# Attention, two mixture-of-experts layers and a feed-forward layer on one core: how the values are loaded, where the row maximum is scaled, and which engine splits two weights

## The chip, the cores and the metric

The kernel runs on one core of a Trainium2 chip. The metric is the device time of one execution in microseconds (us); it includes everything from the first load to the last store.

## The reference

Three layers follow one another on 1536 tokens. First comes attention with 2 x 8 heads of 768 positions and 64 dimensions: each query sees the keys nearer than 16 positions and one summary for each block of 32 positions (the maximum of the keys, the mean of the values). Then every token goes to two of eight experts, and a dense layer with a squared ReLU ends it.

```python
k_sum = k.reshape(B, H, nb, block, D).max(axis=3)
v_sum = v.reshape(B, H, nb, block, D).mean(axis=3)
mask_l = np.abs(pos[:, None] - pos[None, :]) < window            # window 16, block 32
scores_s = scale * np.einsum('bhsd,bhnd->bhsn', q, k_sum) + np.log(block)
a = softmax(concat(where(mask_l, scale * q @ k.T, -1e9), scores_s))
x = a @ concat(v, v_sum)                                         # -> 1536 x 512
# experts: the two largest of 8 noisy logits per token
out[mask] += top2_w[mask, k, None] * (np.maximum(x[mask] @ w1[e], 0) @ w2[e])
# dense layer: s, b scalars
g = s * np.maximum(x @ w_in, 0)**2 + b;  y = g @ w_out
```

## The kernel before

**Attention** is tiled into 8 units, each one pair of heads, and each unit into two groups of 384 queries: 16 groups, n = 0 to 15, group n belonging to unit n // 2. For each unit SyncE's queue issues the loads of the transposed keys (`load_k`), queries (`load_q`) and values (`load_vT`), 128 rows of 768 float32 each, and of the values as the second product reads them (`load_vw`): a tile `VW` of 1560 columns (12 windows x 2 heads x 65, the 65th column holding ones). Of `VW` the rows 0 to 95 come by DMA, as two pieces of 768 columns a row and a third of 24 columns from an array of its own, `v_end`; rows 96 to 120 hold the sums of 24 blocks, which the kernel makes itself, and a row of 1e-9.

A group goes through these stages, each with its own function. `stage_s` (L732 and L735) multiplies queries with the 96 keys of a window and 24 block maxima, in PSUM. `stage_exp` takes the row maximum on VectorE (L742), scales it (L743), and ScalarE forms the exponentials in six instructions (L746). `stage_pt` transposes the result on TensorE (L756) and ScalarE brings it back (L760). `stage_pv` is the product with `VW` (L773), divided on VectorE (L776 and L778). The main loop runs these for groups n, n - 2 and n - 3 side by side. Beside them, for the next unit, `windows` (L709) copies the keys' windows on GpSimd, `block_max` (L713) takes the blocks' maxima on VectorE, and `place_ks` (L717) spreads them on GpSimd. `make_vsum` adds the values of a block: for units 0 to 3 one reduction on VectorE (L688), for units 4 to 7 five additions on GpSimd (L693). `place_vsum` brings the sums into `VW` (L698 on ScalarE, L699 on GpSimd).

Every engine and the SyncE queue run their instructions in the order of the program; that order is written out by hand. `extra(n)` stands at the end of group n: in the even groups it makes the windows of the next unit and issues the loads, `VW` of unit u + 1 first and then keys, queries and values of unit u + 2. A load of `VW` waits until the unit that used its buffer (there are three) is through `stage_pv`. SyncE issues a DMA only when the DMA eight before it has landed.

**The tables.** `CHUNK_AT` says in which groups the first three chunks of expert weights are loaded (`load_chunk`, two DMAs of 512 KB each). `SPLIT_AT` says in which groups `split_step` makes of a weight block a rounded part and a remainder, each for two 128 x 512 halves: ScalarE rounds (L490 and L491), GpSimd subtracts (L492 and L493). The splits 0 and 1 read chunk 0, the splits 2 and 3 chunk 1. `GATE_EV` says whether VectorE (1) or ScalarE (0) takes a transposed token block of the gate out of PSUM (`gate_t`). `ROUTE` spreads the routing of the first half of the tokens, VectorE work for the most part, over groups 12 to 15; it ends with nine comparisons `ohb` (L268). `TAIL` is the order of the work behind the last group, in which the rest of the attention, the routing of the second half (`t`, `u`, `r`, `o`, `i`) and the first expert's steps (`l1`, `l2`) are interleaved; `s.4` there is split 4, `x.1`, `g.5`, `m.1` and `z.1` are a transposition of gathered tokens and the gate. Behind `TAIL` run the experts and the dense layer, where TensorE has no gap.

Of the kernel before, what the change touches and what calls it, by code (L numbers as in the profile page):

```python
# [9 lines left out]
F32 = mybir.dt.float32  # L10
# [9 lines left out]
DRAM = bass.MemoryType.DRAM  # L20

EDGE_CAP = 256
GATE_EV = {(1, 1): 0, (1, 3): 1, (1, 5): 0, (0, 1): 0, (1, 0): 1, (0, 4): 0, (1, 4): 1}
CHUNK_AT = (7, 9, 12)
SPLIT_AT = (12, 13, 14, 15)
SPLIT_DVE = {8: 1, 9: 1, 4: 0}
ROUTE = {12: 2, 13: 3, 14: 7, 15: 6}
GATE = {(10, 0): 't0', (10, 1): 't1', (10, 2): 't2', (11, 0): 't3 m0', (11, 1): 't4', (11, 2): 't5 z0', (12, 0): 'm1', (12, 1): 'z1'}
XT_B = 4
TAIL = ("pt.1 pv.0 d.0 pt.2 pv.1 g.0 g.1 pv.2 g.2 g.3 m.0 x.0 g.4 z.0 x.1 g.5 m.1 l1.0 z.1 l1.1 t.0 s.4 l2.0 l1.2 u.0 c.3 l2.1 s.5 "  # L30
        "r.0 o.7 l2.2 o.2 s.6 l1.3 l1.4 l2.3 o.2 s.7 l1.5 l2.4 c.4 i.0 l1.6 s.8 l1.7 s.9 l2.6 l2.5 p.0 p.1 e.0 p.2 p.3 l2.7 l1.8")
MID_CAPS = (464, 440, 424, 416, 392, 368, 344)


@with_exitstack
def kernel(ctx: ExitStack, tc, q, k, v, v_end, vt_in, w_gate, w_noise, noise, w1, w2,
                      w_in, w_out, s_in, b_in, out):
    nc = tc.nc
    N, Dm = out.shape
    B, H, S, D = 2, 8, N // 2, 64  # L40
# [24 lines left out]
    cp = ctx.enter_context(tc.tile_pool(name="cp", bufs=1))  # L65
# [7 lines left out]
    bk23 = pp.tile([P, 2, 512], F32, name="bk23")  # L73
# [20 lines left out]
    for h in range(2):  # L94
        d = identb[64 * h:64 * h + 64]
# [8 lines left out]
        nc.vector.tensor_copy(masks[kind], masks[0])  # L104
        nc.vector.memset(masks[kind][:, lo:lo + 16], NEG)
    ident = cp.tile([P, P], F32, name="ident")
    zero6 = cp.tile([P, 2, 3], F32, name="zero6")
    wgn = cp.tile([P, DT, 32], F32, name="wgn")
    nz_in = cp.tile([P, B, NI, E], F32, name="nz_in")
    sb_in = cp.tile([P, 2], F32, name="sb_in")  # L110
# [300 lines left out]
    def split_step(n, eng=nc.vector):  # L411
# [11 lines left out]
        split(t, r1[:, :, j * P:(j + 1) * P], r2[:, j], eng)  # L423

# [59 lines left out]
        eng.tensor_tensor(out=v2[:, 1], in0=w, in1=v2[:, 0].bitcast(F32), op=OP.subtract)  # L484


    def split(t, a, bb, eng=nc.vector):

        v4 = t.rearrange("p a (t n) -> p a t n", n=P)
        nc.scalar.activation(v4[:, 0], a, AF.Copy)  # L490
        nc.scalar.activation(t[:, 1], bb, AF.Copy)  # L491
        eng.tensor_tensor(out=v4[:, 2], in0=a, in1=v4[:, 0].bitcast(F32), op=OP.subtract)  # L492
        eng.tensor_tensor(out=t[:, 3], in0=bb, in1=t[:, 1].bitcast(F32), op=OP.subtract)  # L493

# [169 lines left out]
    def win4(t):  # L664
        return t.rearrange("p (j h d) -> p j h d", h=2, d=D + 1)

    def load_k(u):
        kT[u] = kTb[u % 2]
        nc.sync.dma_start(kT[u][:, KPAD:KPAD + S], k[u])

    def load_q(u, eng=nc.sync):
        qT[u] = ap_.tile([P, S], F32, name="qT", bufs=3)
        eng.dma_start(qT[u], q[u])

    def load_vT(u):
# [164 lines left out]
    for t in VW:  # L840
        v4 = win4(t)
        nc.gpsimd.memset(v4[96:KW + 1, :, :, D:D + 1], 1e-9)
        nc.gpsimd.memset(v4[96:KW, :, :, D:D + 1], 32.0)
# [308 lines left out]
    with tc.If(n_over > 0):  # L1152
# [50 lines left out]
```

## Time and profile before

| | |
|---|---|
| three runs | 698.17, 699.72, 700.32 us; median 699.72 us |
| the profiled execution | 702.6 us, of which the span from the first to the last instruction is 700.8 us |
| TensorE, matmuls | 657.2 us busy, 94% of the span |
| VectorE, ScalarE, GpSimd | 441.1, 360.3 and 173.1 us busy |
| granted clock of TensorE | 0.977 of full speed on average |
| DMA | 96 MB in 59,817 packets, of which 7,592 under 512 bytes |

Times in the rows below are microseconds from the start of the span. PE is TensorE's matmuls, PEld its weight loads, DVE VectorE, ACT ScalarE, POOL GpSimd, SPq SyncE's queue. An average over the span says little here: the first 131 us are attention and routing, and the rest is experts and dense layer.

### The profile page before, as it was taken

What the parts mean: (1) busy time and instruction counts of PE and PEld (TensorE: products, weight loads), DVE (VectorE), ACT (ScalarE), POOL (GpSimd) and SP (SyncE); (2) the same over time, 40 slices, a digit from 0 to 9 for tenths busy, and PEclk for the clock granted to TensorE, in tenths of its full rate; (3) what the DMA queues carried; (4) which work ended last, traced back from release to release, by engine and by line L of the source; (5) the groups of instructions that cost most, each with busy time, mean ns of one, the idle gap of its engine ahead of it and who ended that gap; (6) DMA issues with size and microseconds to landing.
All of it is one profiled execution on the core that took longest, in us unless ns stands there. A gap on an engine that the chain in (4) does not pass through costs nothing.

```text
span 700.8 us, 11245 instructions
## 1 busy us (share of the span) xinstructions
PE 657.2 (94%) x4236; PEld 574.0 (82%) x4236; DVE 441.1 (63%) x765; ACT 360.3 (51%) x667; POOL 173.1 (25%) x204
## 2 busy tenths in 40 slices
PE   3796589899999999999999999999999999999995
PEld 3675468788999999999988897888888888888884
DVE  3754938566677677676777766788654565544542
ACT  3684624444545455455656566556454454444431
POOL 5364927403204131221313153610500000000000
PEclk9996789999999999999999999999999999999998
DMA  8898151775556566566667651510410000100001
GB/s 229 246 262 296 63 182 61 235 257 166 189 178 223 194 198 205 192 206 213 220 208 253 225 155 42 178 61 30 121 60 1 1 0 1 60 1 1 0 1 64
DMA packets 59817, 95.99 MB, mean 137 GB/s; under 512 B 7592, under 2 KB 34216, under 8 KB 59756
## 3 DMA queue, kind: packets, MB, share of 16 engines
q1 hardware_dynamic: 55611, 82.02, 36.0%
q0 software_dynamic: 4144, 13.18, 6.8%
q8 instruction: 35, 0.57, 0.3%
q14 instruction: 27, 0.21, 0.1%
HBM read 82.01 MB, written 13.17 MB: 136 GB/s over the span
## 4 chain that ended last, share of the span: by engine, by line
PE 84%; DMA 7%; DVE 5%; SPq 1%; ACT 1%; issue 1%; POOL 0%; DVEq 0%; ACTq 0%; POOLq 0%
PE sbk L499 38%; PE bk L520 24%; PE bk L934 13%; DMA VW<-in_v_dram 3%; PE mbk L526 3%; DMA qT<-in_q_dram 2%; PE mbk L520 1%; PE mbk L965 1%; DMA kT<-in_k_dram 1%; PE bk L773 1%; DVE ohb L268 1%; PE mbk L756 1%; PE mbk L804 1%; DMA xg<-x_d,ids_i 1%; DMA r<-in_moe_w_dram 0%
## 5 line engine op out<-in xcount | busy, mean ns | idle before, releaser
L499 PE MATMUL sbk<-xh,w 128*128 128x512 f32 (+8 forms) x960 | 278.9, 355 | 0.0
L499 PEld LDWEIGHTS sbk<-xh,w 128*128 128x128 f32 x960 | 175.4, 188 | 19.4 <-ACT xh L528 0.4
L499 PE MATMUL sbk<-xl,w 128*128 128x512 f32 (+8 forms) x480 | 170.4, 355 | 0.2 <-DVE xl L529 0.2
L520 PE MATMUL bk<-w,hh 128*128 128x512 f32 (+2 forms) x512 | 161.0, 396 | 0.0
L520 PEld LDWEIGHTS bk<-w,hh 128*128 128x128 f32 (+2 forms) x512 | 93.5, 188 | 17.8
L459 POOL TENSOR_TENSOR cl<-cl,cp 128x512 f32<-128x512 f32 x32 | 41.2, 1289 | 250.5 <-DVE cp L458 234.5
L520 PE MATMUL bk<-w,hl 128*128 128x512 f32 (+2 forms) x256 | 100.5, 392 | 0.0
L499 PEld LDWEIGHTS sbk<-xl,w 128*128 128x128 f32 x480 | 90.3, 188 | 10.3 <-DVE xl L529 0.5
L934 PE MATMUL bk<-hh,w 128*128 128x464 f32 (+4 forms) x320 | 96.3, 362 | 0.0
L490 ACT ACTIVATE w<-r 128x512 fp32r<-128x512 f32 x72 | 45.5, 633 | 85.1 <-PE bk L934 57.8
L492 DVE TENSOR_TENSOR w<-r,w 128x512 fp32r<-128x512 f32 x64 | 44.2, 691 | 37.3 <-ACT w L490 37.0
L510 ACT ACTIVATE yr<-sbk 128x512 f32<-128x512 f32 x48 | 28.7, 598 | 71.2 <-PE sbk L499 71.2
L515 DVE SCALAR_TENSOR_TENSOR hl<-yr,sb_in,hh 128x512 fp32r<-128x512 f32 x48 | 40.0, 833 | 36.0 <-ACT hh L512 36.0
L511 DVE SCALAR_TENSOR_TENSOR yr<-yr,sb_in 128x512 f32<-128x512 f32 x48 | 36.0, 750 | 41.9 <-ACT yr L510 41.9
L934 PEld LDWEIGHTS bk<-hh,w 128*128 128x128 f32 x320 | 59.8, 188 | 2.5
L512 ACT ACTIVATE hh<-yr,sb_in 128x512 fp32r<-128x512 f32 x48 | 34.8, 725 | 45.9 <-DVE yr L511 45.9
L484 DVE TENSOR_TENSOR w<-wres,w 128x1024 fp32r<-128x1024 f32 x36 | 44.1, 1224 | 22.1 <-ACT w L483 22.1
L520 PEld LDWEIGHTS bk<-w,hl 128*128 128x128 f32 (+2 forms) x256 | 47.8, 187 | 11.9 <-DVE hl L515 0.8
L934 PE MATMUL bk<-hl,w 128*128 128x464 f32 (+4 forms) x160 | 56.9, 356 | 0.0
L503 ACT ACTIVATE hh<-sbk 128x256 fp32r<-128x256 f32 (+7 forms) x72 | 34.5, 479 | 42.0 <-PE sbk L499 39.7
L483 ACT ACTIVATE w<-wres 128x1024 fp32r<-128x1024 f32 x39 | 41.3, 1059 | 14.4 <-PE bk L520 9.6
L504 DVE SCALAR_TENSOR_TENSOR hl<-sbk,hh 128x256 fp32r<-128x256 f32 (+7 forms) x72 | 38.9, 541 | 10.5 <-ACT hh L503 10.3
(190 smaller groups left out, 873.9 us busy)
## 6 DMA issues: line engine op xcount, KB each, us to landing
r<-in_moe_w_dram SPq DMA_DIRECT2D x72, 512.0 KB, 4.5
c<-in_moe_w_in_dram SPq DMA_DIRECT2D x16, 512.0 KB, 3.8
c<-in_moe_w_out_dram SPq DMA_DIRECT2D x16, 512.0 KB, 3.7
y_d<-yr SPq DMA_DIRECT2D x23, 256.0 KB, 2.2
VW<-in_v_dram SPq DMA_DIRECT2D x8, 576.0 KB, 11.1
kT<-in_k_dram SPq DMA_DIRECT2D x8, 384.0 KB, 8.3
qT<-in_q_dram SPq DMA_DIRECT2D x8, 384.0 KB, 10.2
xl<-in_vT_dram SPq DMA_DIRECT2D x8, 384.0 KB, 9.8
```

The lines of the kernel that those rows point to most:

```text
L459: nc.gpsimd.tensor_tensor(out=lf, in0=lf, in1=pw.bitcast(F32), op=OP.mult)
L483: nc.scalar.activation(v2[:, 0], w, AF.Copy)
L484: eng.tensor_tensor(out=v2[:, 1], in0=w, in1=v2[:, 0].bitcast(F32), op=OP.subtract)
L490: nc.scalar.activation(v4[:, 0], a, AF.Copy)
L492: eng.tensor_tensor(out=v4[:, 2], in0=a, in1=v4[:, 0].bitcast(F32), op=OP.subtract)
L499: nc.tensor.matmul(ps, wgt[:, t], x[:, t], start=i == 0, stop=i == 3 * DT - 1)
L504: nc.vector.scalar_tensor_tensor(out=hl, in0=ps, scalar=0.0, in1=hh.bitcast(F32), op0=OP.max, op1=OP.subtract)
L511: nc.vector.scalar_tensor_tensor(out=r2, in0=r, scalar=sb_in[:, 0:1], in1=r, op0=OP.mult, op1=OP.mult)
L512: nc.scalar.activation(hh, r2, AF.Identity, bias=sb_in[:, 1:2])
L515: nc.vector.scalar_tensor_tensor(out=hl, in0=r2, scalar=sb_in[:, 1:2], in1=hh.bitcast(F32), op0=OP.add, op1=OP.subtract)
L520: nc.tensor.matmul(a, g, wgt, start=first and j == 0, stop=last and j == 2)
L934: nc.tensor.matmul(a[:, 0:C], wgt[:, c], x[:, 0:C], start=f == 0 and j == 0, stop=last and j == 2)
```

## The change

The values are laid out on the host as 128 whole rows of 1560 columns, with the ones, the 32s and the 1e-9 of column 65 already in them, so that `load_vw` is one DMA of 128 x 1560 float32 instead of two of 96 rows, and the memory sets of these columns on GpSimd fall away. The loads of `VW` go behind the keys, queries and values of the unit after (at the start: behind the keys and queries of units 0 and 1). Rows 96 to 120 are now written by the DMA first and by `place_vsum` after it. The row maximum is written to a few columns of the group's own PSUM bank and scaled from there. All block sums are one reduction on VectorE. Splits 0 and 1 move from groups 12 and 13 to 6 and 8 and run on GpSimd alone; splits 2 and 3 move from groups 14 and 15 into `TAIL`. Chunks 0, 1, 2 are loaded in groups 3, 7, 12 instead of 7, 9, 12. Three of the six blocks of the first gate are taken out of PSUM by VectorE instead of ScalarE. The core of the diff:

```diff
-GATE_EV = {(1, 1): 0, (1, 3): 1, (1, 5): 0, (0, 1): 0, (1, 0): 1, (0, 4): 0, (1, 4): 1}
-CHUNK_AT = (7, 9, 12)
-SPLIT_AT = (12, 13, 14, 15)
+GATE_EV = {(0, 1): 1, (0, 3): 1, (0, 5): 1, (1, 0): 1, (1, 3): 1, (1, 4): 1}
+CHUNK_AT = (3, 7, 12)
+SPLIT_AT = (6, 8)
...
-TAIL = ("pt.1 ... g.4 z.0 x.1 g.5 m.1 l1.0 z.1 l1.1 t.0 s.4 ...
+TAIL = ("pt.1 ... g.4 z.0 x.1 s.2 g.5 m.1 l1.0 z.1 s.3 l1.1 t.0 s.4 ...
...
-    def split(t, a, bb, eng=nc.vector):
+    def split(t, a, bb, eng=nc.vector, hi=act_copy):
         v4 = t.rearrange("p a (t n) -> p a t n", n=P)
-        nc.scalar.activation(v4[:, 0], a, AF.Copy)
-        nc.scalar.activation(t[:, 1], bb, AF.Copy)
+        hi(v4[:, 0], a)
+        hi(t[:, 1], bb)
         eng.tensor_tensor(out=v4[:, 2], in0=a, in1=v4[:, 0].bitcast(F32), op=OP.subtract)
         eng.tensor_tensor(out=t[:, 3], in0=bb, in1=t[:, 1].bitcast(F32), op=OP.subtract)
...
     def load_vw(u):
-        nc.sync.dma_start(VW[u % 3][0:96, 0:2 * S].rearrange("p (t n) -> p t n", t=2), v[u].rearrange("t p n -> p t n"))
-        nc.sync.dma_start(VW[u % 3][0:96, 2 * S:], v_end[u])
+        nc.sync.dma_start(VW[u % 3], v[u])
     def make_vsum(u):
-        if u < HP:
-            nc.vector.tensor_reduce(z[:, 96:KW], t, AX.X, OP.add)
-            return
-        w = 16
-        while w:
-            dst = t[:, :, 0:w] if w > 1 else z[:, 96:KW, None]
-            nc.gpsimd.tensor_tensor(out=dst, in0=t[:, :, 0:w], in1=t[:, :, w:2 * w], op=OP.add)
-            w //= 2
+        nc.vector.tensor_reduce(z[:, 96:KW], t, AX.X, OP.add)
...
-        nc.vector.tensor_reduce(mx, ps, AX.X, OP.max, negate=True)
-        nc.vector.scalar_tensor_tensor(out=mx, in0=mx, scalar=SCALE, in1=zero6, op0=OP.mult, op1=OP.add)
+        m = (bk23, bk45)[n % 2][:, 0, 3 * KW:3 * KW + 6].rearrange("p (h i) -> p h i", h=2)
+        nc.vector.tensor_reduce(m, ps, AX.X, OP.max, negate=True)
+        nc.vector.tensor_single_scalar(mx, m, SCALE, op=OP.mult)
...
     load_q(0)
+    load_k(1)
+    load_q(1)
     load_vT(0)
-    load_k(1)
     load_vw(0)
-    load_q(1)
     load_vT(1)
...
-            if 1 <= u < NU - 1:
-                load_vw(u + 1)
             if u + 2 < NU:
                 load_k(u + 2)
                 load_q(u + 2)
                 load_vT(u + 2)
+            if 1 <= u < NU - 1:
+                load_vw(u + 1)
...
-        for c in range(4):
-            if SPLIT_AT[c] == n:
-                split_step(c, nc.gpsimd)
+        if n in SPLIT_AT:
+            split_step(SPLIT_AT.index(n), nc.gpsimd, nc.gpsimd.tensor_copy)
```

In the rows that follow, a number behind a name is a buffer's, and the brackets name what an instruction waits for: DMAHW a landing, PE, DVE, Activation, Pool the engine.

SyncE's queue, the loads of units 2 to 4, before (`r1`, `r2` would be a chunk's two halves; chunk 0 stands 14 rows further down):

```order
L680 DMA VW2_149<-in_v_dram 96x2x768 [waits DMAHW5_49]
L681 DMA VW2_149<-in_v_end_dram 96x24 [waits DMAHW6_49]
L669 DMA kT1_146<-in_k_dram 128x768 [waits DMAHW7_49,DVE_49,Pool_49]
L673 DMA qT_357<-in_q_dram 128x768 [waits DMAHW0_49,PE_49]
L677 DMA xl_152<-in_vT_dram 128x768 [waits DMAHW1_49,DVE_49]
L680 DMA VW0_147<-in_v_dram 96x2x768 [waits DMAHW2_49,PE_49]
L681 DMA VW0_147<-in_v_end_dram 96x24 [waits DMAHW3_49]
L669 DMA kT0_145<-in_k_dram 128x768 [waits DMAHW4_49,DVE_49,Pool_49]
L673 DMA qT_488<-in_q_dram 128x768 [waits DMAHW5_49]
L677 DMA xl_152<-in_vT_dram 128x768 [waits DMAHW6_49,DVE_49]
```

The same place after:

```order
L671 DMA kT1_145<-in_k_dram 128x768 [waits DMAHW3_49,DVE_49,Pool_49]
L675 DMA qT_345<-in_q_dram 128x768 [waits PE_49]
L679 DMA xl_151<-in_vT_dram 128x768 [waits DMAHW6_49,DMAHW5_49,DVE_49]
L682 DMA VW2_148<-in_v_dram 128x1560
L407 DMA r1_412<-in_moe_w1_dram 128x4x256 [waits DMAHW7_49]
L408 DMA r2_413<-in_moe_w2_dram 128x2x512 [waits DMAHW0_49]
L671 DMA kT0_144<-in_k_dram 128x768 [waits DMAHW1_49,DVE_49,Pool_49]
L675 DMA qT_479<-in_q_dram 128x768 [waits DMAHW2_49,PE_49]
L679 DMA xl_151<-in_vT_dram 128x768 [waits DMAHW3_49,DVE_49]
L682 DMA VW0_146<-in_v_dram 128x1560 [waits DMAHW4_49,PE_49]
```

Each `VW` moved behind the three loads of the unit after it, and chunk 0 came in ahead of unit 4's keys.

GpSimd, from the windows of unit 4 (group 6) to those of unit 5 (group 8), before; L699 is `place_vsum`, L693 the block sums:

```order
L709 COPY kw0_143<-kT0_145 128x12x96 [waits DMAHW4_49,PE_49,Pool_49]
L717 COPY kw0_143<-ks_612 128x12x24 [waits DVE_49]
L699 COPY VW0_147<-vs_652 25x24x64 [waits Activation_49,Pool_49]
L693 TENSOR_TENSOR xl_152<-xl_152 128x24x16 [waits DMAHW6_49,Pool_49]
L693 TENSOR_TENSOR xl_152<-xl_152 128x24x8 [waits Pool_49]
L693 TENSOR_TENSOR xl_152<-xl_152 128x24x4 [waits Pool_49]
L693 TENSOR_TENSOR xl_152<-xl_152 128x24x2 [waits Pool_49]
L693 TENSOR_TENSOR vz0_150<-xl_152 128x24 [waits PE_49,Pool_49]
L709 COPY kw1_144<-kT1_146 128x12x96 [waits DMAHW1_49,PE_49]
L717 COPY kw1_144<-ks_754 128x12x24 [waits DVE_49]
```

And after, where L703, L711 and L693 are the windows, the maxima and `place_vsum`:

```order
L703 COPY kw0_142<-kT0_144 128x12x96 [waits DMAHW1_49,PE_49,Pool_49]
L711 COPY kw0_142<-ks_604 128x12x24 [waits DVE_49]
L492 CAST w4_613<-r1_412 128x512 [waits DMAHW7_49]
L493 CAST w4_613<-r2_413 128x512 [waits DMAHW0_49]
L494 TENSOR_TENSOR w4_613<-r1_412,w4_613 128x512 [waits Pool_49]
L495 TENSOR_TENSOR w4_613<-r2_413,w4_613 128x512 [waits Pool_49]
L693 COPY VW0_146<-vs_648 25x24x64 [waits DMAHW4_49,Activation_49,Pool_49]
L703 COPY kw1_143<-kT1_145 128x12x96 [waits DMAHW5_49,PE_49,Pool_49]
L711 COPY kw1_143<-ks_746 128x12x24 [waits DVE_49]
```

Split 0 took the place of the block sums, and `place_vsum` now waits for the landing of its `VW` as well.

## Rows read from the trace of the kernel before

**Rows 1.** Stretches: borders, length, busy us of each engine, granted clock, DMA share, GB/s

```profile
31.65:39.87 8.22, 8.14 (x199) 7.05 (x199) 8.01 (x15) 6.97 (x25) 4.60 (x5) 1.00 0.74 221
55.23:68.70 13.47, 8.65 (x128) 6.77 (x128) 4.78 (x10) 6.73 (x21) 5.06 (x7) 0.59 0.86 273
68.70:82.40 13.70, 10.53 (x189) 9.14 (x191) 12.99 (x39) 9.71 (x30) 12.11 (x14) 0.87 0.35 113
82.40:92.70 10.30, 4.81 (x63) 4.08 (x59) 7.09 (x16) 3.03 (x8) 8.68 (x9) 0.54 0.07 17
131.00:700.00 569.00, 562.41 (x2825) 494.62 (x2823) 359.94 (x571) 293.25 (x480) 100.47 (x84) 0.99 0.39 125
```

**Rows 2.** Chain that ended last, in order of time: start, us, what

```profile
5.36 14.18 DMA VW<-in_v_dram
19.60 11.91 DMA qT<-in_q_dram
45.04 8.51 DMA kT<-in_k_dram
82.48 5.49 DVE ohb L268 x9
```

**Rows 3.** Timeline: start, us, what, idle before and its releaser

```profile
3.87 0.95 DVE L713 TENSOR_REDUCE ks<-kT 128x24 f32<-128x768 f32 x1
15.13 0.68 PE L732 MATMUL bk<-kw,qT 64*64 64x120 f32 x8 [5.21 <-DMA qT<-in_q_dram]
31.65 0.44 PE L732 MATMUL bk<-kw,qT 64*64 64x120 f32 x8 [2.73 <-DMA qT<-in_q_dram]
55.23 0.43 PE L732 MATMUL bk<-kw,qT 64*64 64x120 f32 x8 [0.23 <-POOL kw L717]
```

**Rows 4.** Stretches chosen by what the DMA queue carries, columns as in Rows 1

```profile
8.00:13.00 5.00, 1.07 (x13) 0.45 (x8) 3.87 (x6) 2.31 (x9) 2.06 (x3) 1.00 1.06 237
31.00:33.00 2.00, 1.35 (x39) 1.25 (x40) 1.93 (x4) 0.34 (x2) 1.49 (x2) 1.00 1.03 395
55.00:59.00 4.00, 1.05 (x39) 0.84 (x39) 3.37 (x6) 2.18 (x8) 3.62 (x6) 0.84 1.07 398
60.00:64.00 4.00, 2.94 (x23) 2.15 (x17) 0.00 (x0) 1.78 (x6) 0.00 (x0) 0.50 1.06 267
68.00:70.00 2.00, 2.00 (x26) 1.74 (x19) 1.93 (x10) 0.15 (x1) 1.27 (x2) 0.50 0.88 269
```

**Rows 5.** Scaling and division on VectorE, ns min/median/max; one scaling beside GpSimd

```profile
L743 DVE SCALAR_TENSOR_TENSOR mxs<-mxs,zero x16: 166/186/1307, 10.1 to 80.0; 128x6 f32<-128x6 f32 x16
L778 DVE TENSOR_TENSOR xs<-bk,rc x16: 557/557/558, 24.3 to 94.9; 128x384 f32<-128x384 f32 x16
...
31.08 1.47 POOL L699 COPY VW<-vs 25x1536 f32<-25x1536 f32 x1
31.25 1.31 DVE L743 SCALAR_TENSOR_TENSOR mxs<-mxs,zero 128x6 f32<-128x6 f32 x1
```

**Rows 6.** Groups by line from 31.65 to 39.87: busy us, mean ns, idle before

```profile
L746 ACT ACTIVATE sm<-bk,mxs 128x120 f32<-128x120 f32 x18 | 4.8, 372 | 3.3 <-DVE mxs L743 3.3
L760 ACT ACTIVATE PT<-mbk 121x384 f32<-121x384 f32 x6 | 2.8, 525 | 0.0
...
L688 DVE TENSOR_REDUCE vz<-xl 128x24 f32<-128x768 f32 x1 | 0.9, 944 | 0.0
```

**Rows 7.** VectorE: scalings by line from 66.9 to 88; second routing's comparisons

```profile
L743 DVE SCALAR_TENSOR_TENSOR mxs<-mxs,zero 128x6 f32<-128x6 f32 x3 | 2.3, 780 | 0.1
...
117.97 1.37 DVE L268 TENSOR_SCALAR ohb<-i,lo 128x128 f16<-128x128 f16 x7
```

**Rows 8.** GpSimd by line from 5 to 75, columns as in Rows 6

```profile
L709 POOL COPY kw<-kT 128x1152 f32<-128x1152 f32 x7 | 8.0, 1143 | 30.0 <-DMA kT<-in_k_dram 30.0
...
L492 POOL TENSOR_TENSOR w<-r,w 128x512 fp32r<-128x512 f32 x1 | 1.3, 1267 | 0.0
```

**Rows 9.** Timeline of the tail, ScalarE, between x.1 and m.1

```profile
100.33 0.60 ACT L794 ACTIVATE xt<-mbk 128x512 f32<-128x512 f32 x1
```

More of the change, by code (lines that the diff above doesn't have):

```diff
@@ L29 @@
 XT_B = 4
-TAIL = ("pt.1 pv.0 d.0 pt.2 pv.1 g.0 g.1 pv.2 g.2 g.3 m.0 x.0 g.4 z.0 x.1 g.5 m.1 l1.0 z.1 l1.1 t.0 s.4 l2.0 l1.2 u.0 c.3 l2.1 s.5 "
+TAIL = ("pt.1 pv.0 d.0 pt.2 pv.1 g.0 g.1 pv.2 g.2 g.3 m.0 x.0 g.4 z.0 x.1 s.2 g.5 m.1 l1.0 z.1 s.3 l1.1 t.0 s.4 l2.0 l1.2 u.0 c.3 l2.1 s.5 "
         "r.0 o.7 l2.2 o.2 s.6 l1.3 l1.4 l2.3 o.2 s.7 l1.5 l2.4 c.4 i.0 l1.6 s.8 l1.7 s.9 l2.6 l2.5 p.0 p.1 e.0 p.2 p.3 l2.7 l1.8")
@@ L35, with kernel @@
 @with_exitstack
-def kernel(ctx: ExitStack, tc, q, k, v, v_end, vt_in, w_gate, w_noise, noise, w1, w2,
+def kernel(ctx: ExitStack, tc, q, k, v, vt_in, w_gate, w_noise, noise, w1, w2,
                       w_in, w_out, s_in, b_in, out):
@@ L106 @@
     ident = cp.tile([P, P], F32, name="ident")
-    zero6 = cp.tile([P, 2, 3], F32, name="zero6")
     wgn = cp.tile([P, DT, 32], F32, name="wgn")
@@ L409, in load_chunk, with act_copy, split_step @@
         nc.sync.dma_start(r2, bb[:, f0:f0 + 2 * P, :].rearrange("o (t p) d -> p (o t) d", p=P))
-    def split_step(n, eng=nc.vector):
+    def act_copy(dst, src):
+        nc.scalar.activation(dst, src, AF.Copy)
+    def split_step(n, eng=nc.vector, hi=act_copy):
         if n >= len(steps):
@@ L422, in split_step @@
         j = n % 2
-        split(t, r1[:, :, j * P:(j + 1) * P], r2[:, j], eng)
+        split(t, r1[:, :, j * P:(j + 1) * P], r2[:, j], eng, hi)
     cv = {}
@@ L831 @@
         nc.vector.memset(t[:, :, :, KW:], 1.0)
-    nc.vector.memset(zero6, 0.0)
     windows(0, 0, 6, nc.scalar)
@@ L839 @@
     nc.gpsimd.memset(wgn, 0.0)
[L840 to L843, printed above, removed]
     st = {}
@@ L1157 @@
     main.close()
-_INS = ['q', 'k', 'v', 'v_end', 'vT', 'moe_w_gate', 'moe_w_noise', 'moe_noise', 'moe_w1', 'moe_w2',
+_INS = ['q', 'k', 'v', 'vT', 'moe_w_gate', 'moe_w_noise', 'moe_noise', 'moe_w1', 'moe_w2',
         'moe2_w_in', 'moe2_w_out', 'moe2_s', 'moe2_b']
@@ L1172, in layouts @@
     vp[:, :, 16:16 + S] = v.reshape(NU, 2, S, D)
-    vw = np.ones((NU, 96, NJ, 2, D + 1), v.dtype)
+    vw = np.zeros((NU, 128, NJ, 2, D + 1), v.dtype)
+    vw[:, :96, :, :, D] = 1.0
+    vw[:, 96:120, :, :, D] = 32.0
+    vw[:, 120, :, :, D] = 1e-9
     for j in range(NJ):
-        vw[:, :, j, :, :D] = vp[:, :, 64 * j:64 * j + 96].transpose(0, 2, 1, 3)
-    vw = vw.reshape(NU, 96, -1)
-    return qT, kT, vw[:, :, :2 * S].reshape(NU, 96, 2, S).transpose(0, 2, 1, 3), vw[:, :, 2 * S:], vT
+        vw[:, :96, j, :, :D] = vp[:, :, 64 * j:64 * j + 96].transpose(0, 2, 1, 3)
+    return qT, kT, vw.reshape(NU, 128, -1), vT
 def kernel(**inputs):
@@ L1187 @@
     inputs = dict(inputs)
-    inputs['q'], inputs['k'], inputs['v'], inputs['v_end'], inputs['vT'] = layouts(_np, *(inputs[n] for n in 'qkv'))
+    inputs['q'], inputs['k'], inputs['v'], inputs['vT'] = layouts(_np, *(inputs[n] for n in 'qkv'))
     for name in _INS:
```

## The prediction

> **What bounds the kernel now.** I read the stretches first. From 131 us to the end TensorE is busy 562.4 of 569 us [rows 1]; the change touches nothing there, so whatever it does must show earlier, and a microsecond won ahead of 131 us is won at the end. Next the chain in order of time: its long pieces up to 54 us are loads, 14.2 us behind a `VW`, 11.9 behind queries, 8.5 behind keys [rows 2]. The timeline says the same from TensorE's side: the scores of group 2 begin at 15.13 us after 5.21 us of waiting for queries, group 6 at 31.65 after 2.73 us [rows 3]; GpSimd waits 30 us in all for keys [rows 8]. So the first half is paced by one DMA queue. Only from group 6 to 9 are loads in time: 18 exponentials are three groups, 8.22 us, 2.74 a group, with VectorE busy 8.01 and ScalarE 6.97 of it [rows 1, 6]. [...]
>
> **Why the loads are slow.** The queue is full nearly always, but at two speeds. Where it carries transfers of 128 rows only (keys, queries, values, chunks, stores) it moves 395 to 398 GB/s; where `VW` is among them 237 to 267, and with a `VW` nearly alone 269, at the same busy share of about 1 [rows 4]. The trace does not say which part of `VW` costs that, the 96 rows or the 96-byte pieces of `v_end`; the change removes both. I take 395 for all loads after; the other end is 237, no cure at all, and in between `VW` at 269 with the rest at 395.
>
> [...]
>
> **Part 1, the loads.** A load of keys, queries or values is 128 x 768 x 4 = 0.393 MB, a `VW` 0.799 (0.599 before), a chunk 1.049, the first half's two stores 1.573. Unit 0's keys are in use at 3.87 [rows 3], which at 395 GB/s puts the stream's start at 2.85.
> - Group 2 needs the keys and queries of unit 1, now third and fourth, but VectorE first sums unit 0's values, fifth: 1.966 MB, 7.8 us. Then come three operations of 0.95 each (sum, maximum, block maximum [rows 3, 6]) and the scaling, 0.17 [rows 5]: 10.8, and with the placing on GpSimd 11.4 instead of 15.13.
> - The keys of unit 6 stand behind 13.65 MB in the new order (19 loads of 0.393, five `VW`, two chunks, small ones): 37.4 us. Before it was 12.2 MB, landed at 45.04 + 8.51 = 53.55 [rows 2], some 240 GB/s.
> - The values of unit 7 (they hold up VectorE now, since their sum runs there) stand behind 17.98 MB: 48.4 us.
>
> Single landings trail the stream by a microsecond or two, which I leave in the range.
>
> **Part 2, the pace.** If the loads are in time, a group costs 2.74 [rows 1]. The sum on VectorE for units 4 to 7 adds 0.94 per two groups [rows 6], and the scaling gives back: it takes 0.17 alone and up to 1.31 beside a GpSimd copy, whose end it shares (31.08 + 1.47 against 31.25 + 1.31), while the division, which reads one operand from PSUM, takes 0.557 always [rows 5]. From PSUM the scaling should therefore never wait; I price it at 0.17 to 0.2, and the maximum written into PSUM at its old 0.9. I take 2.85 a group. Groups 2 and 3 run at the lower clock as now (0.68 against 0.43 us for eight matmuls [rows 3]), 3.2 each. Group 10 then starts at 11.4 + 6.4 + 6 x 2.85 = 34.9; 10 and 11 with the gate take 4 each (two ScalarE copies of 0.6 more [rows 9]), so group 12 starts at 43 instead of 55.23. The keys (37.4 and 1.6 for windows and maxima) are earlier. **Gain 12.**
>
> **Part 3, from group 12 to the comparisons' end.** Before: 55.23 to 87.97, 32.7 us [rows 2, 3]. VectorE was busy 4.78 + 12.99 + 5.49 = 23.3 of it [rows 1, 2]. The splits leave GpSimd here, so the three slow scalings lose 1.8 (2.3 less 3 x 0.17), and the nine comparisons fall to what seven cost where GpSimd is quiet for most of them, 1.37: 1.8 instead of 5.5 [rows 7]. That is 17.8, and two sums of 0.94 make it 19.7. VectorE binds here, TensorE need not wait and keeps its clock. End at 43 + 19.7 = 62.7 instead of 87.97. The loads bound it lower: unit 7's values at 48.4 and the part of the VectorE work that stands behind them, some 11 of the 19.7 us by my estimate, give 60. **Gain 13 more, 25 in all.**
>
> **Part 4, the tail.** Split 2 now stands between `x.1` and `g.5`, where ScalarE is on the path: two copies of 128 x 512, 0.6 each by the nearest one [rows 9], 1.2 lost; split 3's copies fit beside `l1`. GpSimd's four subtractions of 1.27 [rows 8] move into the tail beside VectorE's second routing: 0 to 1.5 lost. Against it the stretch from 82.4 to 92.7 ran at a clock of 0.54 [rows 1] with TensorE half idle; without the wait a microsecond comes back. **Net loss 2** (0 to 3).
>
> **Part 5, costs at nothing, with their cover.** Splits 0 and 1 on GpSimd: two copies of 0.6 to 1.3 and two subtractions of 1.27 each [rows 8], about 4 us in groups 6 and 8. The cover is the 2.5 us of GpSimd sums that leave every unit from 4 on and the 30 us it now waits; without it the windows of the next unit are late by up to 4. Their chunk lands by 23.5 us (8.16 MB), ahead of group 6. ScalarE loses eight copies in groups 12 to 15, counted nowhere, since VectorE binds there.
>
> **Sum.** 25 - 2 = 23 us against the profiled 702.6: 679.6. The runs' median lies 2.9 below the profiled execution, so I expect **677**.
>
> **Rivals.**
> - *GpSimd's queue becomes the bound.* `place_vsum` now waits for its `VW`, which lands last of its unit, and the windows of the unit after stand behind it. For: unit 4's `VW` lands at 33.5 us (12.12 MB), split 1 holds GpSimd to about 36, then 1.47 and 1.14 and the maxima [rows 5, 8]: windows of unit 6 at 39.5, against 43 needed. Against: that margin of 3.5. If copies and landings are both slow it costs up to 6: 683.
> - *The loads stay the bound.* At 300 GB/s unit 7's values land at 62.8, and 11 us of VectorE behind them end at 74: a gain of 14 less 2, 688. With `VW` at 269 and the rest at 395, six `VW` (4.79 MB) take 17.8 us instead of 12.1 and unit 7's values land 5.7 later than 48.4: end at 65 instead of 62.7, 679.
> - *Slower.* 96 rows are not the cause, and the mixed rate stays. Then 1.5 MB more stand ahead of unit 6's keys, and unit 7's values land at 2.85 + 17.98 / 0.237 = 78.7, the comparisons end at 90, 2 later than now, and the tail adds 1 to 2: 703. It decides below some 250 GB/s. For: the slow seconds hold more than `VW`. Against: two fast stretches with 128 rows of other sizes [rows 4].
> - *It does nothing.* A gain of some 12 in the loads given back by GpSimd and by a lower clock: 700.
>
> [...]
>
> **How the numbers follow.** Forecast 0.62, GpSimd 0.15, loads 0.13, nothing 0.04, slower 0.06. The forecast's own range is 668 to 684: up to 9 us less if the end comes by the loads (60), the tail loses nothing and the slow routing operations beside GpSimd's splits, not counted above, shrink too; up to 7 more for late landings. With the first two rivals the range is 667 to 690. A difference of 0.3%, 2.1 us, can be told from none: faster 0.91, the same 0.04, slower 0.05.
>
> **What would show it.** Right: the DMA rate in the first 45 us near 390 with no slow stretch; group 2 at 11 to 12, group 12 at 42 to 45, comparisons done at 60 to 66; no scaling above 0.25 us; the clock at 1.0 from 20 us on. Wrong: GpSimd waiting for `VW` with the windows of unit 5 or 6 behind it, VectorE waiting for a unit's values, or a rate below 300.

## The result, and the profile after

The changed kernel takes 688.16 us (median of four runs, 686.93 to 689.10); the kernel before took 698.94 beside it (four runs, 696.65 to 700.32). The ratio is 0.985, with a 95% interval from 0.982 to 0.988. So it is faster by 10.8 us, where 23 were forecast. The profiled execution took 686.93 us, with a span of 685.2, against 702.6 and 700.8 before.

| | before | forecast | after |
|---|---|---|---|
| scores of group 2 begin | 15.13 | 11.4 | 12.77 |
| scores of group 10 begin | 43.52 | 34.9 | 36.90 |
| scores of group 12 begin | 55.23 | 43 | 47.91 |
| the nine comparisons end | 87.97 | 62.7 | 70.48 |
| gather of unit 1 is issued | 123.00 | | 109.67 |
| end of the span | 700.8 | | 685.2 |

The loads first. These lines of the DMA view cover 3 to 33 us of the changed kernel: the rate in 40 equal slices, and the sum.

```profile
GB/s 410 393 356 188 340 406 451 407 395 402 431 462 377 402 418 410 401 401 399 381 433 436 386 367 362 366 395 397 395 385 420 415 420 374 402 407 371 384 444 374
DMA packets 4139, 11.82 MB, mean 394 GB/s; under 512 B 522, under 2 KB 1034, under 8 KB 4133
```

The same of the kernel before:

```profile
GB/s 418 324 266 213 344 311 225 212 203 254 206 255 288 242 238 193 202 238 224 287 365 352 264 238 207 182 215 252 315 352 238 124 101 274 344 179 210 340 414 393
DMA packets 3266, 7.88 MB, mean 263 GB/s; under 512 B 725, under 2 KB 725, under 8 KB 3263
```

In this stretch the two speeds of [rows 4] are one: 394 GB/s, where 395 was forecast.

Yet TensorE's timeline is not as early as the loads allow. Start, length, what, and the idle time before it with its releaser; the first line answers to the second of [rows 3], the second to its fourth:

```profile
12.77 0.68 PE L726 MATMUL bk<-kw,qT 64*64 64x120 f32 x8 [2.21 <-POOL kw L711]
...
47.91 0.44 PE L726 MATMUL bk<-kw,qT 64*64 64x120 f32 x8
...
53.82 0.30 PE L806 MATMUL bk<-ident,lt 96*128 96x96 f32 x1 [2.15 <-ACT sm L741]
...
55.47 0.68 PE L726 MATMUL bk<-kw,qT 64*64 64x120 f32 x8
```

Groups 10, 11, 12 and 13 as stretches, with the columns of [rows 1]:

```profile
36.90:41.64 4.74, 4.33 (x83) 3.60 (x79) 3.77 (x9) 4.38 (x16) 4.62 (x5) 1.00 0.98 285
41.64:47.91 6.27, 5.68 (x105) 4.60 (x104) 3.46 (x7) 3.93 (x14) 2.70 (x3) 1.00 1.03 396
47.91:55.47 7.56, 5.02 (x92) 3.97 (x92) 2.68 (x5) 3.50 (x12) 1.42 (x2) 0.91 0.82 324
55.47:59.18 3.71, 3.71 (x70) 3.24 (x68) 3.42 (x13) 1.02 (x3) 0.59 (x2) 0.71 0.62 217
```

In groups 10 and 11 TensorE is busy for nine tenths of the time (4.33 of 4.74, 5.68 of 6.27) at full clock: it is the bound, with the gate's transposes and products between the scores. In group 12 it waits 2.15 us for ScalarE, VectorE is busy for only 2.68 of 7.56 us, and group 13 runs at a granted clock of 0.71 on average (0.50 up to 57.6 us, 1.00 from there). In the kernel before, groups 10 and 11 were as full:

```profile
43.52:48.66 5.14, 4.75 (x82) 3.78 (x79) 2.24 (x6) 4.50 (x16) 3.93 (x6) 1.00 0.92 289
48.66:55.23 6.57, 5.75 (x105) 4.61 (x104) 1.92 (x3) 3.37 (x9) 1.51 (x2) 1.00 1.03 339
```

VectorE and the scaling, in the places of [rows 2, 5]: the comparisons take 2.27 instead of 5.49, and no scaling is above 0.166.

```profile
68.21 2.27 DVE L267 TENSOR_SCALAR ohb<-i,lo 128x128 f16<-128x128 f16 x9
```

```profile
L738 DVE TENSOR_SCALAR mxs<-bk x16: 164/165/166, 10.8 to 66.7; 128x6 f32<-128x6 f32 x16
```

The tail gives something back. From the comparisons' end to the gather of unit 1, before and after as stretches:

```profile
87.97:123.00 35.03, 31.08 (x295) 26.76 (x296) 21.69 (x65) 13.09 (x28) 16.48 (x17) 0.94 0.37 122
```

```profile
70.48:109.67 39.19, 32.54 (x285) 27.85 (x286) 20.23 (x64) 13.86 (x30) 20.69 (x21) 0.87 0.33 109
```

That is 4.2 us, with 4.2 us more GpSimd work in it and a lower clock. Of these, 2.3 us come back behind the gather: from there to the end of the span it takes 575.5 us, where it took 577.8. From the comparisons' end to the end of the span the loss is 1.9 us (614.7 against 612.8). The second routing's operations with two operands in SBUF now meet the subtractions of the splits on GpSimd. Of these four, the second and third were long before too, at 1.38 and 0.93; the first and the last took 0.21:

```profile
89.49 1.25 DVE L181 TENSOR_TENSOR t<-t,nz_in 128x48 f32<-128x48 f32 x1
...
92.24 1.23 DVE L193 TENSOR_TENSOR sel<-sel,e 128x96 f32<-128x96 f32 x1
...
93.79 1.20 DVE L196 TENSOR_TENSOR oh<-sel,ms 128x96 f32<-128x96 f32 x1
95.03 1.15 DVE L198 TENSOR_TENSOR mm_b<-oh 128x48 bf16<-128x48 f32 x1
```

### The profile page after: what moved, and what is told of

Read it like the earlier page. It is cut to its first block, busy times and chain, and to the rows that moved or that the text cites. A ratio compares the mean times of both kernels' runs of the same rounds, so it can differ in the third digit from the quotient of the medians.

```text
span 685.2 us, 11202 instructions
## 1 busy us (share of the span) xinstructions
PE 653.4 (95%) x4236; PEld 571.8 (83%) x4236; DVE 434.4 (63%) x771; ACT 355.6 (52%) x660; POOL 164.4 (24%) x182
## 4 chain that ended last, share of the span: by engine, by line
PE 90%; DVE 4%; ACT 2%; DMA 1%; issue 1%; POOL 0%; SPq 0%; ACTq 0%; DVEq 0%
PE sbk L501 40%; PE bk L522 25%; PE bk L923 14%; PE mbk L528 2%; PE bk L768 2%; PE mbk L751 2%; PE mbk L522 1%; PE bk L726 1%; PE mbk L954 1%; DMA xl<-in_vT_dram 1%; ACT sm L741 1%; PE mbk L799 1%; DMA xg<-x_d,ids_i 1%; PE mbk L783 1%; DVE xs L773 0%
## 5 line engine op out<-in xcount | busy, mean ns | idle before, releaser
L411 ACT ACTIVATE w<-r 128x512 fp32r<-128x512 f32 x140 | 80.7, 624 | 91.4 <-PE bk L923 56.9
L494 DVE TENSOR_TENSOR w<-r,w 128x512 fp32r<-128x512 f32 x64 | 44.2, 690 | 35.2 <-ACT w L411 34.7
```

What stands on the lines that cost most here:

```text
L411: nc.scalar.activation(dst, src, AF.Copy)
```

## The experiments

"Comparisons" are the nine of the first routing, "the gather" is that of unit 1. Each kernel is the changed one with the edit shown, unless it says otherwise. Where only one execution was taken, its time is given as such.

### Which part of VW made the loads slow

```diff
 # 96 rows
-        nc.sync.dma_start(VW[u % 3], v[u])
+        nc.sync.dma_start(VW[u % 3][0:96], v[u][0:96])
 # end piece
-        nc.sync.dma_start(VW[u % 3], v[u])
+        nc.sync.dma_start(VW[u % 3][:, 0:2 * S], v[u][:, 0:2 * S])
+        nc.sync.dma_start(VW[u % 3][:, 2 * S:], v[u][:, 2 * S:])
```

96 rows: 

> The changed kernel with VW loaded into 96 rows, each as one piece of 1560 numbers; the other rows are written by GpSimd once at the start. No 96-byte pieces. Theory A (the 96 rows are what made the loads slow): the rate in the first 45 us falls to 240 to 300 GB/s, the keys of unit 7 land at 60 us or later instead of 51.3, 693 to 700 us. Theory B (the 96-byte pieces were it): the rate stays at 380 or more, a quarter less of VW is carried, and the time is that of the changed kernel, 686 to 689 us.

End piece: 

> The changed kernel with VW loaded into 128 rows, in two transfers: 1536 numbers of each row, and the last 24 numbers (96 bytes) of each row by itself. Theory A (96 rows): the rate stays at 370 or more and the time at 687 to 690 us. Theory B (96-byte pieces): the rate in the first 45 us falls to 240 to 300, keys of unit 7 at 60 us or later, 693 to 700 us.

Measured: 96 rows 696.39 us (ten runs, ratio to before 0.998, 0.996 to 1.000): nearly all of the gain is gone, though the new order of the loads stands in this run too. End piece 688.65 (0.987, 0.982 to 0.992), as the changed kernel. The DMA view from 3 to 33 us, 96 rows:

```profile
GB/s 393 332 287 209 262 414 428 311 237 207 202 263 365 216 216 206 246 381 401 411 377 397 397 432 297 255 203 201 284 347 395 382 385 389 409 364 220 236 161 226
DMA packets 3376, 9.26 MB, mean 309 GB/s; under 512 B 333, under 2 KB 845, under 8 KB 3373
```

and the end piece:

```profile
DMA packets 4520, 11.55 MB, mean 385 GB/s; under 512 B 957, under 2 KB 1469, under 8 KB 4515
```

The 96-byte pieces cost next to nothing. The 96 rows bring back the second speed of 200 to 260, and the keys of unit 7 land at 59.7 instead of 51.3. Two ways to carry `VW` as two transfers of fewer rows, one execution each:

```diff
-        nc.sync.dma_start(VW[u % 3], v[u])
+        for r in (0, 64):                          # two halves
+            nc.sync.dma_start(VW[u % 3][r:r + 64], v[u][r:r + 64])
 # or
+        for r0, r1 in ((0, 96), (96, 128)):        # 96 and 32
+            nc.sync.dma_start(VW[u % 3][r0:r1], v[u][r0:r1])
```

Two halves: 

> The changed kernel with VW loaded in two transfers of 64 whole rows, 0 to 63 and 64 to 127, one behind the other. [...] Theory B (what counts is whether a transfer's rows divide evenly over the queue's 16 engines in blocks as those of 64 and 128 do): the rate stays at 380 or more.

96 and 32: 

> The changed kernel with VW loaded in two transfers of whole rows, 0 to 95 and 96 to 127: the same rows and bytes as the changed kernel's one transfer. Theory A (rows written at a time): the uneven 96 are followed at once by the 32 that were missing, so the loss is smaller than with 96 rows alone: a rate of 330 to 380 from 3 to 33 us. Theory B (how a transfer of 96 rows is dealt out to the engines): as slow as with 96 rows alone, 300 to 320, and more bytes to carry, so 695 us or more.

Measured: 704.73 and 699.41 us.

```profile
DMA packets 3033, 8.25 MB, mean 275 GB/s; under 512 B 327, under 2 KB 839, under 8 KB 3031
```

```profile
DMA packets 3267, 8.92 MB, mean 297 GB/s; under 512 B 353, under 2 KB 865, under 8 KB 3265
```

The halves carry the changed kernel's rows and bytes in pieces of the same length, and are the slowest of these kernels, at 275 GB/s: theory B of that run, even division, which had the rate stay at 380 or more, is out. From 3 to 33 us the pieces of 6,240 bytes took a median of 445 ns in the halves, 427 with 96 rows and 418 in 96 and 32, beside 239 in the changed kernel. The pieces of 3,072 bytes of the other loads took a median of 124, 124 and 125 ns, beside 121 (means of 158, 146 and 148 beside 128). So it is the pieces of `VW` itself, above all, that become slow.

96 and 32 came out at 297, about where its theory B had it and below what theory A gave it: a transfer of the other 32 rows right behind does not make up for the loss. What holds is that the queue is slower in each of the three kernels whose transfers of `VW` cover fewer than 128 rows: 309, 297 (96 and 32) and 275 GB/s, beside 394. Each rate is that of one execution, and two executions of the kernel before differ by 44 GB/s, so the order among the three is not shown. What makes pieces of the same length slower in a transfer of fewer rows, these runs leave open.

### The loads alone

The kernel before with whole rows and the new order of loads; nothing else changed.

```diff
-        nc.sync.dma_start(VW[u % 3][0:96, 0:2 * S]..., v[u]...)
-        nc.sync.dma_start(VW[u % 3][0:96, 2 * S:], v_end[u])
+        nc.sync.dma_start(VW[u % 3], v[u])
...
-            if 1 <= u < NU - 1:
-                load_vw(u + 1)
             if u + 2 < NU:
                 load_k(u + 2)
                 load_q(u + 2)
                 load_vT(u + 2)
+            if 1 <= u < NU - 1:
+                load_vw(u + 1)
```

> The kernel before with the loads of the changed one alone: VW as one transfer of 128 whole rows, behind keys, queries and values of the unit after. Scaling, sums, splits, chunks and gate copies as before. Theory A (the loads are the main part, and what the rest won is given back at the gate): DMA rate near 390 GB/s, group 12 at 47 to 50 instead of 55.2, the nine comparisons still 5 us or more, 688 to 692 us. Theory B (the loads alone are worth little, VectorE binds): group 12 early, but the end of the comparisons within 3 us of before, 696 to 700 us.

Measured: 689.86 us, ratio 0.988 (0.983 to 0.993), group 12 at 47.22.

```profile
68.89 5.57 DVE L268 TENSOR_SCALAR ohb<-i,lo 128x128 f16<-128x128 f16 x9
```

Theory A, but for the rate: from 3 to 33 us it is 365 GB/s, where 390 was expected, with 1,732 pieces of 32 bytes in this stretch that come later in the changed kernel. The pieces of `VW` are as fast as there, a median of 238 ns. The loads are most of the gain: 8.3 us, where the end-piece kernel beside it won 9.5. Its comparisons end at 74.46, 4.0 later than the changed kernel's, but from there to the gather it needs 35.1 instead of 39.2, and to the end of the span 612.5 instead of 614.7. About half of what the other parts win at the comparisons they lose in the tail.

### The kernel before once more

> The kernel before, unchanged, for a second trace of it. The forecast was made against one profiled execution of 702.6 us, while the runs' median was 699. Theory A: the stretch ahead of 131 us differs from execution to execution by 2 to 5 us with the same loads; then group 12 or the end of the comparisons of this trace stands 2 us or more away from 55.23 and 87.97, and part of the gain that I read from the first trace was that execution's own. Theory B: the executions differ only behind 131 us; then both stand within 0.5 us.

Measured: one execution, 693.38 us. Its DMA rate from 3 to 33 us, and its comparisons:

```profile
GB/s 418 397 385 381 381 221 262 232 325 410 389 176 258 237 279 393 415 381 303 213 245 255 287 376 382 382 283 270 241 270 263 274 402 397 250 262 244 249 228 261
DMA packets 3847, 9.21 MB, mean 307 GB/s; under 512 B 883, under 2 KB 883, under 8 KB 3841
```

```profile
73.71 5.57 DVE L268 TENSOR_SCALAR ohb<-i,lo 128x128 f16<-128x128 f16 x9
```

Theory A: with the same loads the rate was 307, not 263, and the comparisons end at 79.28, not 87.97. Both traces are of one kernel, so the 8.7 us lie in the execution. The kernel before scatters from 693.4 to 702.7 us over all its runs here, and the one profiled for the forecast was among its slowest.

### What sets groups 10 to 13

Three edits. The gate of group 12 later:

```diff
-... (11, 2): 't5 z0', (12, 0): 'm1', (12, 1): 'z1'}
+... (11, 2): 't5 z0', (12, 1): 'm1', (13, 0): 'z1'}
-ROUTE = {12: 2, 13: 3, 14: 7, 15: 6}
+ROUTE = {13: 5, 14: 7, 15: 6}
```

> The changed kernel with the last gate product of the first half moved behind the exponentials of group 12 and its transpose behind the scores of group 13; the first routing begins a group later with as many steps in all. Theory A (with the loads cured the gate holds the groups up: TensorE's transpose of the gate waits 2.15 us for exponentials of group 12, which stand on ScalarE behind the gate's copy): scores of group 13 at 51 to 53 us instead of 55.5, no low clock there, comparisons' end 2 to 4 us earlier than 70.4. Theory B (the loads still bind there): scores of group 14 stay at 58 to 60 behind the keys of unit 7, comparisons' end within 1 us of 70.4.

Measured: one execution of 683.62 us. TensorE:

```profile
47.91 0.43 PE L726 MATMUL bk<-kw,qT 64*64 64x120 f32 x8
...
52.03 0.44 PE L726 MATMUL bk<-kw,qT 64*64 64x120 f32 x8
...
57.75 0.68 PE L726 MATMUL bk<-kw,qT 64*64 64x120 f32 x8 [2.83 <-DVE z_all L182]
```

Group 12 shrinks from 7.56 to 4.12 us. But group 14 waits 2.83 for the routing's first operations, which read the gate's part of the same PSUM tile, and the low clock has moved there (0.68 on average from 58 to 63 us); the comparisons end at 68.85, 1.6 earlier and not the 2 to 4 of theory A. Timed on another chip:

> The changed kernel with the gate of group 12 later and nothing else, timed on the same chip. If the one look of 683.6 holds: 683 to 686 us, 3 to 5 less than the changed kernel's 688. If that look was a lucky execution: 686 to 689.

Measured: 686.97 us (686.08 to 687.32), ratio 0.984 (0.979 to 0.989), so the first figure was one of its best. Its group 2 begins 0.7 later, and from group 12 to the comparisons' end it takes 21.1 us, beside 20.9 in the first execution and 22.6 in the changed kernel. The wait in group 12 costs about 1.5 us in this stretch; as a time of the whole kernel it is not clear of the noise (0.984 beside 0.985).

A later chunk:

```diff
-CHUNK_AT = (3, 7, 12)
+CHUNK_AT = (3, 12, 12)
```

> The changed kernel with the second weight chunk loaded in group 12 instead of 7, so that 1.05 MB less, 2.6 us at 400 GB/s, stand ahead of the keys of units 6 and 7. Theory A (the gate binds in groups 10 to 13): the keys of unit 7 land 2 to 3 us earlier than 51.3, but scores of groups 11, 12, 13 and the comparisons' end stay within 1 us of 41.6, 47.9, 55.5 and 70.4. Theory B (the loads bind): groups 12 and 13 and the comparisons' end come 2 to 3 us earlier.

Measured: one execution of 688.47 us. The keys of unit 6 land at 38.8, 3.4 earlier, and those of unit 7 at 50.1, 1.2 earlier; groups 11, 12, 13 begin at 42.74, 49.02, 56.01 and the comparisons end at 71.65. Nothing is earlier (the whole execution began 0.6 later). The loads do not bind there any more.

Gate transposes issued twice:

```diff
         xp = bank()
-        for t in range(DT):
-            nc.tensor.transpose(...)
+        for _ in range(2 - b):
+            for t in range(DT):
+                nc.tensor.transpose(...)
```

> The changed kernel with every one of the six gate transposes of the first half issued twice into the same bank (24 more, 0.59 us more for each token block; three blocks in group 10, three in group 11). Theory A (TensorE sets groups 10 and 11, since it is busy for 4.3 of 4.7 and 5.7 of 6.3 us there, and my forecast left its gate work out): group 10 takes 1.2 to 2.0 us longer, group 11 too, and the comparisons end 2 to 4 us later. Theory B (evacuations of the gate and loads set these groups): each group longer by less than 0.6 us, comparisons' end within 1 us.

Measured: one execution of 688.18 us. Groups 10 and 11:

```profile
36.92:42.93 6.01, 5.65 (x95) 4.92 (x91) 4.21 (x10) 4.77 (x16) 5.72 (x6) 1.00 0.96 319
42.93:50.51 7.58, 6.99 (x117) 5.92 (x116) 3.37 (x7) 4.12 (x12) 2.22 (x3) 1.00 1.04 408
```

1.27 and 1.31 us longer than in the changed kernel, TensorE busier by 1.32 and 1.31, and the comparisons 2.2 later, at 72.67. Theory A: in these two groups what TensorE gets to do is paid in full.

### Where the splits stand

Splits 2 and 3 in groups 12 and 13, on GpSimd alone:

```diff
-SPLIT_AT = (6, 8)
+SPLIT_AT = (6, 8, 12, 13)
-TAIL = ("... z.0 x.1 s.2 g.5 m.1 l1.0 z.1 s.3 l1.1 ...
+TAIL = ("... z.0 x.1 g.5 m.1 l1.0 z.1 l1.1 ...
```

> The changed kernel with splits 2 and 3 back ahead of the tail, on GpSimd alone like the first two, in groups 12 and 13. Theory A (in the tail they cost 3 us: two ScalarE copies on the path of the gate, and four subtractions beside VectorE's second routing, whose short operations take 1.2 instead of 0.2 us): from the comparisons' end to the gather of unit 1 37 us instead of 39.3, and the end 2 to 3 us earlier, 684 to 686 us. Theory B (GpSimd's work beside the first routing costs as much as it wins): comparisons' end 1.5 to 3 us later, 687 to 689.

Measured: one execution of 687.89 us. Both theories, each for its stretch: the comparisons end at 73.59, 3.1 later, and from there to the gather it takes 34.9, 4.3 less (2.2 less to the end of the span). With the gate moved as well:

> Both edits in one: gate of group 12 later, splits 2 and 3 in groups 12 and 13. If both theories A hold, 681 to 684 us; if the gains exclude each other (GpSimd's splits beside the routing that now comes later), 685 to 688.

Measured: 685.06 us, ratio 0.982 (0.977 to 0.986); the comparisons end at 72.03, 34.7 to the gather. The gains partly exclude each other, as the second case said. So the gate later, and the splits where GpSimd waits for loads:

```diff
-SPLIT_AT = (6, 8, 12, 13)
+SPLIT_AT = (6, 8, 10, 11)
```

> The changed kernel with the gate of group 12 later, as in the run that gave 683.6, and with splits 2 and 3 in groups 10 and 11, on GpSimd alone, where it waits for the keys of unit 6 and the values of unit 5; the splits then stand neither beside the first routing nor in the tail. Theory A (the splits cost where VectorE has operations with two operands in SBUF, and nothing elsewhere): comparisons' end at 68 to 70 us, 35 us from there to the gather of unit 1, 678 to 682 us. Theory B (GpSimd becomes the bound: windows of unit 7 at 51.4 and the placing of unit 5's sums at 46.4 are pushed back by up to 4 us): comparisons' end at 72 to 74, 683 to 686 us.

Measured: 683.06 us (682.89 to 685.10), ratio 0.979 (0.974 to 0.984), and 3.9 less than the kernel with the gate alone, on the same chip. Comparisons' end and gather as a stretch, and two of the second routing's operations:

```profile
70.20:104.26 34.06, 29.67 (x295) 25.50 (x296) 21.63 (x65) 12.97 (x28) 16.20 (x17) 1.00 0.38 125
```

```profile
87.37 0.21 DVE L181 TENSOR_TENSOR t<-t,nz_in 128x48 f32<-128x48 f32 x1
...
91.38 0.21 DVE L198 TENSOR_TENSOR mm_b<-oh 128x48 bf16<-128x48 f32 x1
```

Theory A for the stretches (the comparisons' end is 0.2 late), with the time 1 us above its range. The tail's loss is the splits': without them it takes 34.1 us at a clock of 1.00, with them 39.2 at 0.87. It holds to the end of the span: every trace here with the splits 2 and 3 in the tail takes 613.1 to 616.9 us from the comparisons' end to there, every other 610.6 to 612.8. This version has the lowest median here, ahead of both kernels.

### Sums and scaling undone

The sums of units 4 to 7 back on GpSimd:

```diff
-        nc.vector.tensor_reduce(z[:, 96:KW], t, AX.X, OP.add)
+        if u < HP: (the reduction) else: (five nc.gpsimd.tensor_tensor additions)
```

> The changed kernel with the block sums of units 4 to 7 back on GpSimd as five additions. Theory A (in the changed kernel neither engine binds in groups 6 to 11, TensorE and the gate do): scores of group 12 within 1 us of 47.9, and the sums of 0.94 that VectorE saves show nowhere ahead of group 12; behind it the end moves by less than 1 us. Theory B (GpSimd is short of time, since splits 0 and 1 stand there now): group 10 or 12 is 1.5 to 4 us late, 688 to 691 us.

Measured: one execution of 693.09 us, comparisons' end at 76.37 instead of 70.48. GpSimd around split 1 (behind the new additions, L694, its line numbers are 7 higher than the changed kernel's: L710 is the windows, L718 the maxima):

```profile
36.13 2.47 POOL L694 TENSOR_TENSOR xl<-xl 128x384 f32<-128x384 f32 x4
...
38.85 1.14 POOL L710 COPY kw<-kT 128x1152 f32<-128x1152 f32 x1
39.93 0.42 POOL L718 COPY kw<-ks 128x288 f32<-128x288 f32 x1
40.30 0.61 POOL L492 CAST w<-r 128x512 fp32r<-128x512 f32 x1
40.86 0.61 POOL L493 CAST w<-r 128x512 fp32r<-128x512 f32 x1
41.44 1.26 POOL L494 TENSOR_TENSOR w<-r,w 128x512 fp32r<-128x512 f32 x1
```

and TensorE, which waits for the sums:

```profile
38.95 0.57 PE L761 MATMUL mbk<-ident,vz 128*121 128x128 f32 x1 [2.12 <-POOL vz L694]
```

Theory B: the row of GpSimd's operations has no gap, and VectorE's 0.94 a unit buys some 5 us, by this one execution. The sums' move is what lets splits 0 and 1 lie in groups 6 and 8 for nothing.

The scaling back in SBUF:

```diff
-        nc.vector.tensor_reduce(m, ps, AX.X, OP.max, negate=True)
-        nc.vector.tensor_single_scalar(mx, m, SCALE, op=OP.mult)
+        nc.vector.tensor_reduce(mx, ps, AX.X, OP.max, negate=True)
+        nc.vector.scalar_tensor_tensor(out=mx, in0=mx, scalar=SCALE, in1=zero6, op0=OP.mult, op1=OP.add)
```

> The changed kernel with the maxima scaled from SBUF with two operands again. Theory A (both forms wait for the same thing only beside a GpSimd copy with which they share an end; GpSimd's copies still meet some of them): mean of the scaling 0.3 to 0.6 us instead of 0.17, some above 1 us, group 12 and the comparisons' end 0 to 2 us later. Theory B (what shortened the scaling was the work that left GpSimd, not PSUM): mean below 0.2 us, no difference.

Measured: one execution of 688.08 us, comparisons' end at 71.21.

```profile
L738 DVE SCALAR_TENSOR_TENSOR mxs<-mxs,zero 128x6 f32<-128x6 f32 x16 | 5.2, 325 | 0.5
```

The mean doubles to 0.325, 2.6 us in all. The comparisons end 0.7 us later, and the time of this one execution lies among those of the changed kernel: theory A's durations, and the lower part of its range. Five of the sixteen scalings take 0.38 to 1.17 us; with the splits out of groups 12 to 15 only two of them stand behind group 12, where VectorE is full.

## Why the prediction was wrong, and where it was right

Direction and first mechanism held: the loads were the bound, and a cure of the queue brings 394 GB/s (395 forecast). The size was wrong: 23 us were forecast and 10.8 came. That 688 lies inside the range is luck, since its upper end of 690 stood for two rivals that did not come about. Three steps failed, all about what binds and from where to count once the loads are cured. Part 2 gave the gate's work on TensorE in groups 10 and 11 no price (3.0 us). Part 3 held that VectorE binds and TensorE need not wait (2.9 us). The sum took one slow execution as its base (4.1 us). Step by step:

- **The bound and the cure.** Right. The loads alone give 8.3 us. Which part of `VW` costs the rate was left open, and the change removes both; it is the 96 rows.
- **Part 1, landings.** Group 2 came 1.4 us late: the values behind which VectorE waits landed at 8.96, not 7.8. The keys of unit 6 came at 42.22 instead of 37.4 and the values of unit 7 at 53.25 instead of 48.4. The sign "near 390 with no slow stretch" held to 33 us only: from 33 to 45 us the mean was 270 GB/s, and the queue ran nearly dry (50 and 47 GB/s in the two microseconds from 34 to 36). By the run with the late chunk that cost nothing.
- **Part 2, the pace: the gate's work on TensorE was left out.** Groups 2 to 9 took 24.1 us, forecast 23.5. "10 and 11 with the gate take 4 each" failed: 4.74 and 6.27. I had priced only ScalarE's copies. Each token block's transposes take some 0.66 us on TensorE's timeline, the product of the gate in group 11 takes 1.07, and TensorE was full there. The run with doubled transposes shows it paid one for one: in group 10, 1.32 us more work and 1.27 us more time. That is 3.0 us; with 0.6 for the pace and 1.4 from the start, group 12 is 4.9 late.
- **Part 3: the bound and the cover of TensorE failed.** 22.6 us from group 12 to the comparisons' end instead of 19.7, the sum of VectorE's work. VectorE was busy for 16.8 of the 22.6: it is full from group 13 on (14.2 of 15.0 us) and idle for most of group 12. The comparisons fell as said, 5.49 to 2.27 (1.8 forecast), and it was the splits' leaving: with the old scaling they stay at 2.27. But "TensorE need not wait and keeps its clock" did not hold: the gate's transpose waits 2.15 us behind exponentials and the clock falls to 0.71 in group 13. Moving it saves 1.5 of the 2.9 us.
- **Part 4, the tail.** Its place, causes and size were right: to the end of the span 1.9 us are lost where 2 (0 to 3) stood. Up to the gather it is 4.2 us: the splits' subtractions stretch more of the routing's operations, and the expected microsecond from a better clock went the other way, 0.94 to 0.87. What gives 2.3 of it back behind the gather no run singles out.
- **Part 5, costs at nothing.** Right, and the cover is what the prediction named: with the sums back on GpSimd it costs 5 us.
- **The scaling.** Its mechanism was right, 0.165 us always. Part 2 sets it against the new sums; undone, it costs 0.7 us at the comparisons' end in one execution, and nothing of the time that is clear of the noise.
- **The sum: the wrong execution as a base.** In the profiled executions the gain is 15.6 us of the span (17.5 to the comparisons' end, less 1.9), not 23. Then "the runs' median lies 2.9 below the profiled execution" was carried over to the kernel after. The second trace of before shows that such an excess lies ahead of the comparisons, where the loads ran at 263 instead of 307 GB/s, and this is the stretch that the change cures; after has its profiled execution 1.2 below its median. This last step alone is 4.1 of the 11.2 us between 677 and 688.16.

The rivals: GpSimd did wait, 2.84 us for a `VW` and 3.25 for keys, but TensorE was busy meanwhile, so its queue did not bind. The loads did not stay the bound. The time, 688, is that rival's by chance; it came about otherwise.

## What to carry to other kernels

When one bound is lifted, add up the busy time of every other engine stage by stage, not only of the engine that the change touches: the next bound was TensorE's own gate work, readable in the trace of before (busy 4.75 of 5.14 and 5.75 of 6.57 us). Load whole sets of 128 rows even where a quarter of them is padding, as here (394 GB/s, against 309 with 96 rows), and if the loads' rate scatters, take the base of a forecast from more than one execution. Work that is moved off one path is not gone: put it where its engine waits and where it does not run beside VectorE operations such as those here with two operands in SBUF, of which one took 1.25 us beside a GpSimd subtraction and 0.21 without.

## What the runs showed of the hardware

- Transfers of `VW` into fewer than 128 rows slow the queue, at a DMA share still near 1 (1.01 to 1.03 for the queue, beside 1.02): 394 GB/s with 128 rows, 309 with 96, 275 with twice 64, from 3 to 33 us. Their own pieces of 6,240 bytes take 427 and 445 ns instead of 239. A transfer of the missing 32 rows right behind does not mend it (297), and 96-byte pieces cost next to nothing (385).
- The kernel before scatters from 693.4 to 702.7 us. Whether that goes with its slow loads is not shown: with 96 rows ten runs lie within 4.3 us, with whole rows sets of four runs within 1.2 to 4.5.
- A VectorE operation of 128x48 numbers took 1.25 us beside a GpSimd subtraction and 0.21 without; the scaling that reads PSUM took 0.164 to 0.166 us sixteen times of sixteen.
